# Moving one table-load step of ScalarE from the end of a recurrent-attention and feed-forward kernel to its front

## The chip, the cores and the metric

One NeuronCore of a Trainium2 chip runs the kernel. The metric is the device time of one execution in microseconds. A core has five engines that run side by side, each through its own list of instructions in order: TensorE (PE, matrix products), VectorE (DVE), ScalarE (ACT, functions such as exponential, and copies), GpSimd (POOL, here a few elementwise steps and the issue of most loads) and SyncE (SP, here the issue of stores and of transposing DMAs). Engines wait for each other through semaphores.

## The reference

Two stages. The first is a recurrent attention with a decay for every channel, for 4 batches, 8 heads, 768 steps and 48 channels a head:

```python
for t in range(S):
    cur = np.einsum('bhd,bhe->bhde', u[None] * kt, vt)
    y[:, :, t] = np.einsum('bhd,bhde->bhe', rt, state + cur)
    state = wt[:, :, :, None] * state + np.einsum('bhd,bhe->bhde', kt, vt)
```

The second takes y as x, with 3072 rows (batch and step) and 384 columns, through a gated feed-forward block with 1024 inner channels:

```python
a = x @ w1
b = x @ w2
h = a * b @ w3
return (h @ w_out).astype(np.float32)
```

## The kernel before

The 768 steps are cut into 6 chunks of 128, and the work into 13 units (`UNITS`): unit t is one chunk of one or two batches. Inside a chunk the recurrence becomes matrix products. For that the kernel needs products of decays over many steps, which it forms as exponentials of running sums of logarithms. So each unit t has, on ScalarE, one logarithm and then three or four exponentials:

- `ln_t` (line 401): lw = ln(w), as soon as the unit's w (`win_t`) has landed
- `cs_t` on TensorE (lines 413, 418): running sums of lw, by a product with a triangular matrix of ones; `csT_t` (line 450) the same, transposed, for units 0, 2, 3 and 6
- `pc_t` (line 425), `ne_t` (line 432), and `iw_t` and `e_t` (lines 471, 479) or, for units 0, 2, 3 and 6, `et_t` (line 456): exponentials of these sums or of lw

From these VectorE scales k and r (`KRk_t` line 437, `KRw_t` line 467, `KRr_t` line 483), TensorE or a transposing DMA on SP turns them (`trk_t`, `trr_t`, `dtk_t`, `dtr_t`), TensorE forms the products inside the chunk (`m_t_b`, line 548), VectorE masks them (`msk_t_b`, line 567; for a few, ScalarE copies in `mcp_t_b` and GpSimd or VectorE masks), and TensorE makes y from them and from the state (`yi_t_b` line 593, `ys_t` line 583). VectorE adds the term in u (`yb_t`, line 611), and y is transposed into `xT` (`yt_t` and `xT_t`, or `dty_t_b`).

The feed-forward block of unit t follows: `a_t_g` and `b_t_g` (line 687) are x times w1 and w2, ScalarE copies a out (`asb_t_g`, line 692), VectorE multiplies it by b (`abT_t_g`, line 697), and `o_t_b` (line 703) multiplies by `w34`, which is w3 times w_out, formed once in the kernel (`wt`, `w3Te`, `wm`, `w34e`, lines 364 to 378). `osb_t_b` (line 708) copies the result out and `st_t_b` (line 713) stores it.

No scheduler sets the order of the work. It is written out by hand in `ORDER`: each entry is a step's name and the engine that runs it, and every engine runs its own entries in that order. `warmN@n` entries are n matmuls of zeros (line 301), 59 in all in the first 35 us. `BANKS` says which banks of the matrix-product memory and which buffers each step uses; a step that writes a bank waits until the step that read it before is done. Loads of r, k, v, w and of the weights are issued by GpSimd (line 328 and lines 339 to 354).

ScalarE computes a logarithm or an exponential from a table that must be in place. The program builder puts a table load (`ACT_TABLE_LOAD`, `LoadActFuncSet` in the built program) before each function that the table in place doesn't hold; it bears the line of that function. The table that it picks for a logarithm has no exponential, and the one that it picks for an exponential has no logarithm. Copies need none of their own. The step `table` (line 238) loads, by name, a table that has both. In the kernel before it follows `asb_10_0`, with 13 of ScalarE's 154 steps behind it: all logarithms and exponentials stand ahead of it.

Of the kernel before, what the change touches and what calls it, by code (L numbers as in the profile page):

```python
# [58 lines left out]
sa12_0=0 o11_1=2 so11_0=1 o12_1=3 so11_1=3 o12_0=4 so12_1=1 so12_0=3  # L59
"""  # L60
ORDER = """
zeros@DVE vin_0@SP padr@DVE win_1@POOL rin_0@SP padlw@DVE ones@DVE mask1@DVE kin_0@SP win_0@POOL u@SP kin_1@POOL
win_2@POOL rc_0@DVE LT@POOL rin_2@POOL rin_1@POOL ln_1@ACT warm0@18 cs_1@PE vin_1@POOL kc_0@DVE ln_0@ACT padkr@DVE
I128@POOL w3_0@POOL warm1@7 trw_0@PE cs_0@PE csT_0@PE pc_0@ACT win_3@POOL ne_0@ACT KRk_0@DVE padet@DVE mask@POOL
ln_2@ACT kin_2@POOL et_0@ACT warm4@13 csT_2@PE pc_1@ACT iw_1@ACT trk_0@PE KRw_0@DVE uc@POOL trw_2@PE ne_1@ACT cs_2@PE
rk_1@DVE kin_3@POOL trke_0@DVE pc_2@ACT e_1@ACT rw_1@DVE KRk_1@DVE ne_2@ACT KRr_1@DVE w3_1@POOL warm1@5 kv_1@PE
ruk_1@DVE trr_1@PE rk_0@DVE m_0_0@PE rin_3@POOL trk_1@PE msk_0_0@DVE trke_1@ACT trre_1@ACT wo@POOL wt_1_0@PE ruk_0@DVE
et_2@ACT warm6@1 wt_1_1@PE dg_0@DVE m_1_0@PE vc_0@DVE wt_0_0@PE msk_1_0@DVE dv_0@POOL warm4@1 wt_0_1@PE ln_3@ACT
kv_0@PE win_4@POOL KRw_2@DVE w3Te_0@ACT warm5@3 cs_3@PE rk_2@DVE vin_2@POOL pc_3@ACT warm7@1 csT_3@PE ne_3@ACT
KRk_2@DVE dg_1@DVE warm7@1 trk_2@PE et_3@ACT w3_2@POOL ruk_2@DVE yi_0_0@PE trke_2@DVE dv_1@POOL yi_1_0@PE w3Te_1@DVE  # L70
vin_3@POOL warm7@2 yd_1@PE S_1@DVE KRk_3@DVE warm7@2 m_2_1@PE S_0@DVE mcp_2_1@ACT warm7@1 trk_3@PE ybc_1@DVE wt_3_0@PE
trke_3@ACT warm2@1 wt_3_1@PE maff_2_1@DVE yt_1@PE wt_2_0@PE trw_3@PE yb_0@DVE wt_2_1@PE KRw_3@DVE m_2_0@PE yt_0@PE
mcp_2_0@ACT rk_3@DVE m_3_0@PE xT_1@ACT maff_2_0@POOL m_3_1@PE msk_3_1@DVE w1_1@POOL warm2@7 wm_1@PE msk_3_0@DVE
rin_4@POOL dg_2@DVE wm_0@PE w3Te_3@ACT kin_4@POOL w34e_1@DVE ln_4@ACT wm_3@PE win_5@POOL w3Te_2@DVE Sb_0@ACT
w34e_0@ACT dv_2@DVE w2_1@POOL yi_2_0@PE cs_4@PE Sb_1@DVE kin_5@POOL yi_2_1@PE pc_4@ACT wm_2@PE ne_4@ACT yb_2@DVE
w1_0@POOL e_4@ACT ruk_3@DVE wt_5_0@PE wt_4_0@PE w34e_3@ACT wt_5_1@PE ys_3@PE xT_0@ACT w3Te_5@DVE yt_2@PE rin_5@POOL
yi_3_0@PE dg_3@DVE xT_2@ACT wt_4_1@PE wm_5@PE iw_4@ACT dv_3@DVE vin_4@POOL w3Te_4@ACT yi_3_1@PE a_0_1@PE yb_3@DVE
w34e_5@ACT a_2_3@PE rw_4@DVE w3_3@POOL yt_3@PE KRr_4@DVE a_2_2@PE trr_4@PE rk_4@DVE asb_2_2@ACT w2_0@POOL wm_4@PE
trre_4@DVE asb_2_3@ACT ruk_4@DVE xT_3@DVE kv_3@PE ln_5@ACT win_7@POOL kv_2@PE a_1_1@PE KRk_4@DVE w34e_4@ACT dg_4@DVE
cs_5@PE asb_0_1@ACT trk_4@PE pc_5@ACT S_2@DVE iw_5@ACT win_6@POOL b_0_1@PE T_3@DVE ne_5@ACT b_2_2@PE abT_0_1@DVE  # L80
S_3@POOL b_3_2@PE e_5@ACT KRk_5@DVE kin_6@POOL a_3_2@PE asb_1_1@ACT abT_2_2@DVE Sb_2@ACT b_1_1@PE asb_3_2@ACT
rin_6@POOL b_2_3@PE abT_1_1@DVE trke_4@ACT a_1_0@PE abT_2_3@DVE m_4_0@PE abT_3_2@DVE m_4_1@PE mcp_4_0@ACT a_3_0@PE
rw_5@DVE a_0_0@PE KRr_5@DVE asb_1_0@ACT Sb_3@DVE trr_5@PE msk_4_1@DVE maff_4_0@POOL asb_0_0@ACT a_2_1@PE a_3_3@PE
trre_5@DVE win_8@POOL asb_2_1@ACT rk_5@DVE ys_4@PE trk_5@PE dv_4@DVE vin_5@POOL yi_4_0@PE trke_5@ACT wt_6_0@PE
yi_4_1@PE a_3_1@PE yb_4@DVE rin_7@POOL wt_6_1@PE b_0_0@PE ruk_5@DVE kin_7@POOL w3Te_6@DVE b_1_0@PE dty_4_0@SP
abT_0_0@DVE b_2_1@PE win_9@POOL abT_1_0@DVE asb_3_1@ACT wt_7_0@PE dty_4_1@SP wm_6@PE ln_7@ACT abT_2_1@DVE dg_5@DVE
asb_3_0@ACT b_3_0@PE w34e_2@ACT ln_6@ACT vin_6@POOL b_3_1@PE abT_3_0@DVE asb_3_3@ACT wt_7_1@PE abT_3_1@DVE cs_6@PE
kv_4@PE pc_6@ACT ne_6@ACT m_5_1@PE T_4@DVE rin_8@POOL a_2_0@PE msk_5_1@DVE iw_7@ACT csT_6@PE asb_2_0@ACT b_3_3@PE
KRk_6@DVE cs_7@PE w3Te_7@DVE win_10@POOL trk_6@PE pc_7@ACT w34e_6@DVE ne_7@ACT b_2_0@PE trke_6@DVE S_4@POOL a_4_1@PE
et_6@ACT abT_3_3@DVE trw_6@PE abT_2_0@DVE e_7@ACT kin_8@POOL b_4_0@PE KRw_6@DVE asb_4_1@ACT ys_5@PE rk_6@DVE m_5_0@PE  # L90
ln_8@ACT m_6_0@PE win_11@POOL msk_5_0@DVE wm_7@PE mcp_6_0@ACT iw_8@ACT rw_7@DVE vin_7@POOL cs_8@PE KRr_7@DVE yi_5_0@PE
w34e_7@ACT a_4_0@PE dv_5@DVE pc_8@ACT ne_8@ACT rin_9@POOL a_4_3@PE ruk_6@DVE asb_4_0@ACT yi_5_1@PE o_0_0@PE Sb_4@DVE
abT_4_0@DVE yb_5@DVE ln_9@ACT vin_10@POOL o_2_0@PE asb_4_3@ACT dg_6@DVE e_8@ACT rin_10@POOL o_3_0@PE osb_0_0@DVE
iw_9@ACT rk_7@DVE st_0_0@SP dtr_7@SP rw_8@DVE kin_9@POOL yt_5@PE osb_3_0@ACT b_4_1@PE osb_2_0@DVE xT_5@ACT ruk_7@DVE
st_3_0@SP kv_6@PE KRr_8@DVE kv_5@PE m_6_1@PE abT_4_1@DVE maff_6_0@POOL ys_6@PE ln_10@ACT a_5_2@PE dtr_8@SP T_5@DVE
b_4_3@PE vin_9@POOL S_5@DVE asb_5_2@ACT msk_6_1@DVE yi_6_0@PE st_2_0@SP a_5_3@PE win_12@POOL a_5_1@PE T_6@DVE
asb_5_3@ACT KRk_8@DVE cs_9@PE KRk_7@DVE yi_6_1@PE dtk_8@SP a_4_2@PE abT_4_3@DVE vin_8@POOL b_5_3@PE rk_8@DVE
asb_5_1@ACT dv_6@DVE b_5_1@PE ln_11@ACT o_3_1@PE pc_9@ACT iw_10@ACT yb_6@DVE kin_10@POOL ne_9@ACT abT_5_3@DVE yt_6@PE
b_4_2@PE dg_7@DVE asb_4_2@ACT a_5_0@PE e_9@ACT abT_5_1@DVE rin_12@POOL trk_7@PE xT_6@DVE asb_5_0@ACT b_5_0@PE rw_9@DVE
# [18 lines left out]
asb_9_2@ACT st_6_1@SP abT_9_3@DVE st_7_1@SP dtk_12@SP b_9_1@PE osb_8_1@ACT ys_11@PE abT_9_1@DVE st_7_0@SP m_11_0@PE  # L118
m_11_1@PE dtr_12@SP ruk_12@DVE o_8_0@PE msk_11_0@DVE b_9_2@PE msk_11_1@DVE yi_11_0@PE b_10_3@PE osb_8_0@DVE a_10_0@PE
dg_12@DVE a_10_2@PE abT_9_2@DVE yi_11_1@PE dv_12@POOL a_10_3@PE yb_11@DVE a_10_1@PE dty_11_1@SP b_10_1@PE asb_10_1@ACT  # L120
b_10_2@PE asb_10_3@ACT asb_10_2@ACT dty_11_0@SP abT_10_3@DVE o_9_1@PE abT_10_1@DVE asb_10_0@ACT st_8_0@SP table@ACT
m_12_0@PE osb_9_1@DVE m_12_1@PE ys_12@PE msk_12_0@DVE o_9_0@PE msk_12_1@DVE b_10_0@PE b_11_2@PE abT_10_2@DVE
yi_12_0@PE a_11_2@PE b_11_0@PE asb_11_2@ACT yi_12_1@PE osb_9_0@ACT a_11_0@PE yb_12@DVE b_11_3@PE abT_10_0@DVE
dty_12_0@SP a_11_1@PE abT_11_2@DVE b_11_1@PE asb_11_1@ACT dty_12_1@SP o_10_0@PE asb_11_0@ACT st_9_0@SP o_10_1@PE
osb_10_0@ACT a_12_1@PE osb_10_1@DVE a_12_3@PE abT_11_1@DVE st_10_1@SP st_8_1@SP b_12_1@PE abT_11_0@DVE st_10_0@SP
st_9_1@SP a_11_3@PE b_12_0@PE asb_11_3@ACT b_12_2@PE asb_12_1@ACT abT_11_3@DVE asb_12_3@ACT a_12_2@PE b_12_3@PE
asb_12_2@ACT a_12_0@PE abT_12_2@DVE o_11_0@PE abT_12_3@DVE asb_12_0@ACT abT_12_0@DVE o_11_1@PE abT_12_1@DVE
osb_11_0@ACT st_11_0@SP o_12_1@PE osb_11_1@DVE st_11_1@SP o_12_0@PE osb_12_1@ACT st_12_1@SP osb_12_0@ACT st_12_0@SP
"""


# [631 lines left out]
```

## Time and profile before

| | |
|---|---|
| time, median of 3 runs | 186.27 us (185.09 to 186.48) |
| profiled execution, its own time | 186.57 us |
| its span, first to last instruction | 184.8 us |
| TensorE busy | 165.1 us (89%) |
| VectorE busy | 135.1 us (73%) |
| ScalarE busy | 115.3 us (62%) |
| GpSimd busy | 82.6 us (45%) |
| table loads on ScalarE | 21, of 1283 ns each |

Busy times are sums over the span; the span and the time differ by what lies before the first and after the last instruction. An instruction's idle time is the time that its engine stood still just before it, and the releaser is what ended that wait. In groups and timelines, L401 is line 401 of the kernel.

### The profile page before, as it was taken

What the parts mean: (1) busy time and instruction counts of PE and PEld (TensorE: products, weight loads), DVE (VectorE), ACT (ScalarE), POOL (GpSimd) and SP (SyncE); (2) the same over time, 40 slices, a digit from 0 to 9 for tenths busy, and PEclk for the clock granted to TensorE, in tenths of its full rate; (3) what the DMA queues carried; (4) which work ended last, traced back from release to release, by engine and by line L of the source; (5) the groups of instructions that cost most, each with busy time, mean ns of one, the idle gap of its engine ahead of it and who ended that gap; (6) DMA issues with size and microseconds to landing.
All of it is one profiled execution on the core that took longest, in us unless ns stands there. A gap on an engine that the chain in (4) does not pass through costs nothing.

```text
span 184.8 us, 4729 instructions
## 1 busy us (share of the span) xinstructions
PE 165.1 (89%) x1981; PEld 122.4 (66%) x1985; DVE 135.1 (73%) x219; ACT 115.3 (62%) x174; POOL 82.6 (45%) x82
## 2 busy tenths in 40 slices
PE   7997769979989996989699999599999969999992
PEld 2454446548778975856478878377678848797860
DVE  4425976758868977897989898489998867751560
ACT  2387985399698479899969748945433410723421
POOL 7997470998252986998703020031277103000000
PEclk9999999999999999999969999999999999999999
DMA  5999999999999999999999929053499993303413
GB/s 120 220 167 203 175 227 189 82 184 188 171 227 190 121 135 148 173 169 143 192 142 176 168 49 161 1 142 63 112 65 135 62 273 101 85 4 85 170 55 117
DMA packets 99669, 25.83 MB, mean 140 GB/s; under 512 B 91712, under 2 KB 97472, under 8 KB 99648
## 3 DMA queue, kind: packets, MB, share of 16 engines
q0 software_dynamic: 76320, 15.96, 98.3%
q1 hardware_dynamic: 23328, 9.57, 25.6%
q8 instruction: 15, 0.25, 0.6%
q14 instruction: 6, 0.05, 0.1%
HBM read 27.98 MB, written 4.72 MB: 177 GB/s over the span
## 4 chain that ended last, share of the span: by engine, by line
PE 58%; ACT 24%; DMA 7%; issue 5%; DVE 2%; POOL 1%; SPq 0%; ACTq 0%; DVEq 0%; POOLq 0%
PE banks L687 26%; PE banks L703 14%; ACT L401 4%; DMA win<-in_w_dram 4%; DMA out_dram<-osb 4%; ACT a_sb L692 3%; PE banks L548 3%; ACT lw L401 3%; PE banks L593 2%; PE banks L301 2%; PE banks L373 2%; PE banks L413 2%; ACT NEt L432 2%; ACT L425 1%; ACT ETt L456 1%
## 5 line engine op out<-in xcount | busy, mean ns | idle before, releaser
L687 PE MATMUL banks<-xT,w_bf 128*128 128x256 bf16 (+1 forms) x624 | 71.2, 268 | 0.7 <-ACT Et L479 0.7
L687 PEld LDWEIGHTS <-w_bf 128*128 128x128 bf16 x624 | 55.8, 99 | 8.4 <-issue 1.1
L692 ACT COPY a_sb<-banks 128x512 f32<-128x512 f32 x48 | 27.3, 590 | 32.0 <-PE banks L687 25.0
L697 DVE TENSOR_TENSOR abT<-a_sb,banks 128x512 bf16<-128x512 f32 x48 | 31.8, 682 | 10.5 <-ACT a_sb L692 6.9
L703 PE MATMUL banks<-w,abT 128*128 128x384 bf16 x192 | 33.9, 326 | 0.9 <-ACT w L378 0.9
L703 PEld LDWEIGHTS <-abT 128*128 128x128 bf16 x192 | 18.2, 98 | 11.7 <-issue 0.9
L567 DVE TENSOR_TENSOR Mbf<-banks,mask 128x1024 bf16<-128x1024 f32 x19 | 22.7, 1220 | 3.1 <-PE banks L548 3.0
L536 POOL TENSOR_TENSOR dv<-vin,dg 128x768 bf16<-128x768 bf16 (+1 forms) x7 | 9.1, 1294 | 35.3 <-DVE dg L527 21.0
L301 PE MATMUL banks<-zeros 128*128 128x512 bf16 x59 | 17.9, 431 | 1.6 <-DVE zeros L242 1.2
L708 ACT COPY osb<-banks 128x384 f32<-128x384 f32 x17 | 7.9, 479 | 14.5 <-PE banks L703 11.5
L328 POOL DMA_DIRECT2D win<-in_w_dram x13 | 15.0, 1153 | 3.8 <-ACT lw L401 1.9
L611 DVE TENSOR_TENSOR yb<-banks,dv 128x768 bf16<-128x768 f32 (+1 forms) x12 | 11.1, 922 | 6.2 <-PE banks L593 3.2
L328 POOL DMA_DIRECT2D rin<-in_r_dram x12 | 13.8, 1154 | 1.0 <-DVE rk L517 1.0
L328 POOL DMA_DIRECT2D kin<-in_k_dram x12 | 14.0, 1164 | 0.2 <-issue 0.2
L328 POOL DMA_DIRECT2D vin<-in_v_dram x12 | 13.8, 1147 | 0.3 <-issue 0.3
L401 ACT ACTIVATE lw<-win 128x768 bf16<-128x768 f32 (+1 forms) x13 | 10.3, 795 | 5.4 <-DMA win<-in_w_dram 5.3
L401 ACT ACT_TABLE_LOAD x10 | 12.8, 1283 | 1.4 <-PEq L747 0.8
L662 POOL TENSOR_TENSOR Sst<-Tst,pc 128x384 f32<-128x384 f32 x4 | 3.7, 918 | 19.7 <-DVE Tst L654 19.7
L301 PEld LDWEIGHTS <-zeros 128*128 128x128 bf16 x63 | 6.3, 107 | 8.3 <-issue 3.5
L527 DVE TENSOR_REDUCE dg<-ruk 128x16 f32<-128x768 bf16 (+1 forms) x13 | 11.4, 884 | 0.0
L373 PE MATMUL banks<-wo_bf,w3T 128*128 128x384 bf16 x64 | 11.4, 326 | 0.0
L548 PE MATMUL banks<-KRT 64*128 64x128 bf16 x192 | 8.3, 217 | 3.1 <-ACT a_sb L692 2.2
(89 smaller groups left out, 242.7 us busy)
## 6 DMA issues: line engine op xcount, KB each, us to landing
out_dram<-osb SPq DMA_DIRECT2D x24, 192.0 KB, 2.1
win<-in_w_dram POOLq DMA_DIRECT2D x11, 384.0 KB, 8.3
rin<-in_r_dram POOLq DMA_DIRECT2D x11, 192.0 KB, 9.6
kin<-in_k_dram POOLq DMA_DIRECT2D x11, 192.0 KB, 7.6
vin<-in_v_dram POOLq DMA_DIRECT2D x11, 192.0 KB, 9.3
w_bf<-in_moe_w_dram POOLq DMA_DIRECT2D x4, 512.0 KB, 9.6
w_bf<-in_moe_w_dram POOLq DMA_DIRECT2D x4, 384.0 KB, 8.7
wo_bf<-in_moe_w_out_dram POOLq DMA_DIRECT2D x1, 768.0 KB, 12.5
```

Source lines behind the costliest of these rows:

```text
L301: nc.tensor.matmul(banks[:, at, :], lhsT=zeros[:, :C], rhs=zeros, start=True, stop=True)
L328: QUEUE[eng].dma_start(dst, src)
L373: nc.tensor.matmul(one(f"wm{fi}")[:, :DM], lhsT=w3T[fi % 2][:, gi, :], rhs=wo_bf[:, gi, :], start=(gi == 0), stop=(gi == FI - 1))
L401: nc.scalar.activation(LW[:, :, :D], ww, Act.Ln)
L527: nc.vector.reduce_sum(dgs, ruks, axis=AX.X)
L548: nc.tensor.matmul(o[:, e, q, :], lhsT=KRTs[a:a + PAD, 0, b * HP + q, :], rhs=KRTs[a:a + PAD, 1, b * HP + q, :], start=True, stop=True)
L567: nc.vector.tensor_mul(Mbf[bank[f"M{t}_{b}"]], mview(), mask.rearrange("s (j q) t -> s j q t", j=2))
L611: nc.vector.tensor_add(ybs.rearrange("t b (q e d) -> t e (b q) d", e=2, d=D), yview().rearrange("t e (x d) -> t e x d", d=D), dvs.rearrang ...
L687: nc.tensor.matmul(o[:, f, :], lhsT=wt[:, di, fi * P:(fi + 1) * P], rhs=x[:, di, :T], start=(di == 0), stop=(di == DI - 1))
L692: copier(eng)(a_sb[bank[f"sa{t}_{g}"]], one(f"a{t}_{g}"))
L697: nc.vector.tensor_mul(ab[:, g * per:(g + 1) * per, :T], sa.rearrange("p (f t) -> p f t", t=T), one(f"b{t}_{g}").rearrange("p (f t) -> p f ...
L703: nc.tensor.matmul(one(f"o{t}_{b}")[:, :DM], lhsT=ab[:, fi, b * C:(b + 1) * C], rhs=w34[:, fi, :], start=(fi == 0), stop=(fi == FI - 1))
```

## The change

One entry of `ORDER`, `table@ACT`, moves from between `st_8_0@SP` and `m_12_0@PE` to the very front. No other entry changes place; the rest of the diff is the same text with its line breaks shifted.

```diff
 ORDER = """
-zeros@DVE vin_0@SP padr@DVE win_1@POOL rin_0@SP padlw@DVE ones@DVE mask1@DVE kin_0@SP win_0@POOL u@SP kin_1@POOL
-win_2@POOL rc_0@DVE LT@POOL rin_2@POOL rin_1@POOL ln_1@ACT warm0@18 cs_1@PE vin_1@POOL kc_0@DVE ln_0@ACT padkr@DVE
+table@ACT zeros@DVE vin_0@SP padr@DVE win_1@POOL rin_0@SP padlw@DVE ones@DVE mask1@DVE kin_0@SP win_0@POOL u@SP
+kin_1@POOL win_2@POOL rc_0@DVE LT@POOL rin_2@POOL rin_1@POOL ln_1@ACT warm0@18 cs_1@PE vin_1@POOL kc_0@DVE ln_0@ACT
...
-b_10_2@PE asb_10_3@ACT asb_10_2@ACT dty_11_0@SP abT_10_3@DVE o_9_1@PE abT_10_1@DVE asb_10_0@ACT st_8_0@SP table@ACT
-m_12_0@PE osb_9_1@DVE m_12_1@PE ys_12@PE msk_12_0@DVE o_9_0@PE msk_12_1@DVE b_10_0@PE b_11_2@PE abT_10_2@DVE
+b_10_2@PE asb_10_3@ACT asb_10_2@ACT dty_11_0@SP abT_10_3@DVE o_9_1@PE abT_10_1@DVE asb_10_0@ACT st_8_0@SP m_12_0@PE
+osb_9_1@DVE m_12_1@PE ys_12@PE msk_12_0@DVE o_9_0@PE msk_12_1@DVE b_10_0@PE b_11_2@PE abT_10_2@DVE yi_12_0@PE
...
```

In the built programs the lists of TensorE, VectorE, GpSimd and SyncE are the same. ScalarE's list differs in its table loads alone. Before there are 21: ten at line 401, six at line 425, two at line 479, and one each at lines 456, 471 and 238. After there is one, at line 238, as ScalarE's first instruction. The line of each source statement stays the same.

## The prediction

> **What bounds the kernel now.** The page comes first: TensorE is busy for 165.1 of 184.8 us, and ScalarE's busiest slices are the ones in which TensorE's digit falls.
>
> ```profile
> PE 165.1 (89%) x1981; PEld 122.4 (66%) x1985; DVE 135.1 (73%) x219; ACT 115.3 (62%) x174; POOL 82.6 (45%) x82
> PE   7997769979989996989699999599999969999992
> ACT  2387985399698479899969748945433410723421
> PEclk9999999999999999999969999999999999999999
> ```
>
> One slice is 4.6 us. From slice 3 to slice 24 ScalarE is mostly at 8 or 9 tenths and TensorE mostly below its full 9; after 120 us ScalarE falls to 1 to 5 tenths and TensorE stays full. So there are two regimes: up to about 120 us ScalarE holds TensorE up at places, after it TensorE sets the time alone.
>
> Then ScalarE's groups, shapes kept apart, for what it does there (line, engine, operation, count; busy us, mean ns; idle before).
>
> ```profile
> L401 ACT ACT_TABLE_LOAD x10 | 12.8, 1283 | 1.4 <-PEq L747 0.8 <-DMA win<-in_w_dram 0.5
> L425 ACT ACT_TABLE_LOAD x6 | 7.7, 1283 | 0.1
> L479 ACT ACT_TABLE_LOAD x2 | 2.6, 1283 | 0.0
> L456 ACT ACT_TABLE_LOAD x1 | 1.3, 1283 | 0.0
> L471 ACT ACT_TABLE_LOAD x1 | 1.3, 1283 | 0.0
> L238 ACT ACT_TABLE_LOAD x1 | 1.3, 1283 | 0.0
> ```
>
> Twenty-one loads, 26.9 of ScalarE's 115.3 us. They stand wherever a logarithm (L401) follows an exponential or the other way round; L238 is the step that is moved.
>
> Third, TensorE's waits, of which the four longest on ScalarE are these (total us, times, longest).
>
> ```profile
> PE banks L548 <- ACT a_sb L692: 2.2, 1, 2.2
> PE banks L413 <- ACT lw L401: 1.8, 3, 1.1
> PE banks L413 <- ACT w L378: 1.1, 1, 1.1
> PE banks L462 <- ACT ETt L456: 1.1, 1, 1.1
> ```
>
> The timeline shows what stands behind the first of them.
>
> ```profile
> 114.63 1.28 ACT L401 ACT_TABLE_LOAD   x1
> 115.92 0.84 ACT L401 ACTIVATE lw<-win 128x768 bf16<-128x768 f32 x1
> 116.67 0.46 ACT L708 COPY osb<-banks 128x384 f32<-128x384 f32 x1
> 117.15 1.28 ACT L479 ACT_TABLE_LOAD   x1
> 118.45 0.81 ACT L479 ACTIVATE Et<-banks 128x768 bf16<-128x768 f32 x1
> ...
> 119.79 0.40 PE L548 MATMUL banks<-KRT 64*128 64x128 bf16 x8 [2.16 <-ACT a_sb L692]
> ```
>
> Two loads stand within 4 us, ScalarE runs without a pause, and TensorE idles 2.16 us until the copy behind them has emptied a bank. On the chain that ended last, table loads stand at twelve places and take 14.1 us (11.19, 13.35, 20.78, 23.84, 37.05, 48.93, 51.94, 66.48, 80.83, 84.61, 87.24 and 117.15 us): a ceiling, since other work comes up as they go.
>
> **What the change does to the instructions.** In the built programs ScalarE has 21 loads before and one after; nothing else moves on any engine, and no DMA or queue is touched. The load at 0.79 us is replaced by the joint one in the same place, also 1283 ns by the L238 row. It is hidden by the 4.01 us that ScalarE idles before 6.09 us for win; without that cover it would cost 1.28. The load at 159.61 lies ahead of a 3.22 us wait for TensorE (to 164.12): nothing. So 19 loads, 19 x 1.283 = 24.4 us of ScalarE, lie where they can matter. A load starts only after the wait of the instruction it serves (at 11.19 ScalarE first waits 0.46 for win), so idle time before it doesn't hide it.
>
> **What each stretch gives.** I go by TensorE's idle times as the timeline puts them, and ask at each whether ScalarE, without its loads and with TensorE already early by the sum so far, is done in time.
>
> To 20 us: idle 0.19 (13.38) and 1.06 (15.29, for et_0). Without the loads ln_2 runs 11.2 to 12.0 when win lands, and et_0 ends at 12.6 instead of 15.24; the warm matmuls keep TensorE until 13.19. Both go: 1.25. The 0.67 at 19.40 stays: there ScalarE itself had waited 1.07 for TensorE.
>
> 20 to 34: 0.16 and 0.49 before cs_3 and 0.92 at 26.06 (for ne_3) go; of 0.56 at 26.98 (for et_3) 0.21 goes, since et_3 itself (1.03) follows ne_3 directly; 0.47 at 32.63 stays (the copy waited for TensorE). 1.78, together 3.03.
>
> 34 to 60: 1.07 at 39.85 (w34e_0 behind the load at 37.05), 0.15 (51.12), 0.71 (55.60), 0.14 (57.89). With loads gone at 37.05, 39.82, 48.93 and 51.94 ScalarE is early by 5 us at e_5. 2.07, together 5.10.
>
> 60 to 92: 1.15 (70.26, ln_6), 0.55 (72.93, ne_6), 0.85 (83.39, w34e_7 behind 80.83), 0.59 (89.39, e_8 behind 87.24), 1.02 (91.20, xT_5). Six loads, 7.7 us, leave a ScalarE that is without a pause from 66.5 to 91.2 but for 0.69. All go; 0.23 at 79.96, ended by VectorE, stays. 4.16, together 9.26.
>
> 92 to 118: TensorE has no idle time, so loads at 97.55 and 114.63 give nothing by themselves. Two things meet here. The granted clock is at half for 3.4 us:
>
> ```profile
> 90.00:100.00 10.00, 8.98 (x100) 6.93 (x95) 8.73 (x14) 8.12 (x13) 1.91 (x3) 0.83 1.65 166
> ```
>
> The three closing columns are granted clock, DMA share and GB/s: 0.83 over 10 us is 1.7 us of matmul time lost (twelve 128x256 matmuls take 2.41 at 91.49, 1.47 at 75.00). It follows three idle times within 8 us that the change removes, so up to 1.7 may come back. Against it, VectorE idles only 1.00 (84.62) between 75.3 and 96.9, so it is early by 6.7 + 1.0 = 7.7 where TensorE is early by 9.26: TensorE would wait up to 1.3 for msk_6_1 ahead of yi_6_0 (93.69 before). VectorE then has 5.44 us of idle (0.87, 0.37, 0.81, 0.62, 2.77) to catch up by 119.3. Between -1.7 and +1.3 I take 0.
>
> By the Trainium skill ("TensorE: Matmul & The Clock Gate", section "HAM oscillation — how this bites in real kernels") the clock falls after idle gaps of over about 3.4 us. The trace differs: the longest idle time in the 20 us before 91.88, where the clock falls, is 1.02. By that rule the half-clock stretch has another cause and may stay; the sum, which counts no clock, would be the same and its lower end 1.7 higher.
>
> At 119.79 the 2.16 go: without 2.57 us of loads osb_5_1, e_10 and asb_7_0 end ahead of TensorE. Together 11.42.
>
> After 120: TensorE's 1.18 (150.00, a transposing DMA) and 0.32 (150.98, a copy behind a store) stay. Nothing.
>
> The sum: 11.4 us. Profiled execution 186.57 (span 184.8 and 1.8 around it, unchanged) - 11.4 = 175.2; the median shown is 0.3 lower, so 174.9.
>
> **Loads from memory** could stop this, since the load queue's packets fill 98.3% of the engines' time. Even with no landing earlier than now it holds: w2's second half lands at 46.2 and is first read at 52.1 (5.9 to spare, 4.25 needed there), w2's first half 56.2 and 63.9 (7.7, needed 5.1), win_6 60.0 and 69.4 (9.4, needed 5.1 to 6.3).
>
> **Rivals.**
> VectorE takes the bound from 75 us on and doesn't give it back: the gain stops at 6.8 + 1.0 = 7.8, 178.5 us. For it: 9 tenths in many slices from 60 to 140 us. Against: its later idle times wait for TensorE or ScalarE, which both come earlier.
>
> Stores and transposing DMAs on SP come forward by 9 to 11 us, into the stretch where the load queue is still busy (last landing 107.8 in that run of loads). A KR transpose issue takes 2.99 at 94.95 and 1.24 at 108.77; a store lands in 6.85 at 143.52 against a median of 2.1. One such landing more on the path costs 4.75: 179.6. Against: the transposes of units 8 and 9 (issued at 94.95 to 110.72) are first read from 119.79 and 132.29 on, over 20 us later.
>
> On the other side: logarithm and exponential are slower out of the joint table, of which no row here has one. Lines 401, 425, 432, 456, 471 and 479 spend 40.2 us in 59 activations. Were each twice as long, ScalarE would have 40.2 - 24.4 = 15.8 us more, and at the 11.4 / 24.4 = 0.47 that a microsecond of ScalarE is worth above, the kernel would be 7.4 slower: 193.7. It decides from 61% longer (24.4 / 40.2). Against: 768 elements take 845 ns as logarithm and as exponential (L401, L471) from two different tables, so the shape sets it.
> The Trainium skill ("ScalarE activation tables: per-element evaluation and per-set limits", section "What a function is on this engine") says that the same operands cost the same whichever table is read, and the two rows agree; by that rule this rival has no chance.
>
> That the loads stay: the built program has none left, so 186.3 only if the order of instructions didn't hold on the chip.
>
> **How the numbers follow.** Forecast 0.70, VectorE 0.15, SP's DMAs 0.10, slower activations 0.02, loads stay 0.01, the rest spread over smaller gains 0.02. Range: down to 174.9 - 1.7 (clock back in full) - 0.4 (what is left at 26.98) = 172.8, up past both rivals to 180.5. Faster by over 1% (what a measurement here can tell from no change, 1.9 us) 0.95; within 1% 0.03; slower 0.02.
>
> **What would show it.** One table load on ScalarE and 24 to 26 us less busy time; logarithm and exponential still near 845 ns; TensorE's waits on ScalarE down from 13.1 to under 3 us; the 2.16 before L548 gone; no half-clock slice near 90 us. It is wrong if TensorE's total idle stays over 12 us, if VectorE's tiles (KR, Mbf, abT) head its waits, or if lw, NEt or Et rows have grown.

## The result, and the profile after

| | before | after |
|---|---|---|
| median (range) of 4 runs each | 185.81 us (185.09 to 186.48) | 178.99 us (177.10 to 180.47) |
| profiled execution: time, span | 186.57, 184.8 us | 180.47, 178.8 us |

The ratio is 0.960, with a 95% interval of 0.950 to 0.970: faster, by some 7 us where the prediction had 11.4. Here and below, medians and ranges are of all executions, while a ratio leaves out those more than 1.5% above the fastest of their kernel. The time lies inside its range (172.8 to 180.5), nearer to the rivals' times (178.5 and 179.6) than to the forecast's 174.9. The profiled execution is the longest of its four, so its losses are at the upper end of what this kernel loses.

The page of the changed kernel, in the same lines as before (engines; busy tenths in 40 slices of 4.5 us; granted clock; the two DMA queues with packets, MB and share of the 16 engines):

```profile
PE 163.7 (92%) x1981; PEld 121.6 (68%) x1985; DVE 133.8 (75%) x219; ACT 89.0 (50%) x154; POOL 82.5 (46%) x82
PE   7998998999999997999999799919999889999991
ACT  2255853586774578964791774222623312232431
PEclk9999999999999999999999999996999999999999
q0 software_dynamic: 76320, 15.96, 103.4%
q1 hardware_dynamic: 23328, 9.57, 30.5%
```

ScalarE is busy 26.3 us less and is no longer at 9 tenths for long. But TensorE has a new hole: slice 26, from 116 to 121 us, holds a 1 where before there was a 9, and the slice of half clock has moved behind it. TensorE's waits and VectorE's (total us, times, longest) name the hole:

```profile
PE banks L703 <- ACT osb L708: 3.8, 1, 3.8
PE banks L687 <- DMA xT<-yb: 1.4, 2, 1.2
...
PE banks L630 <- DVE yb L611: 1.1, 1, 1.1
```

```profile
DVE rw L475 <- DMA rin<-in_r_dram: 4.5, 1, 4.5
...
DVE KR L437 <- DMA kin<-in_k_dram: 1.3, 1, 1.3
```

The timeline of that stretch (start, us, engine, line, tiles; in brackets the idle time before it and what ended it) shows how one leads to the other:

```profile
115.34 1.46 PE L703 MATMUL banks<-w,abT 128*128 128x384 bf16 x8
118.32 0.56 DVE L475 TENSOR_TENSOR rw<-rin,iw 128x768 bf16<-128x768 bf16 x1 [4.51 <-DMA rin<-in_r_dram]
118.80 1.02 DVE L437 TENSOR_TENSOR KR<-kin,NEt 128x768 bf16<-128x768 bf16 x2
...
119.38 0.81 ACT L432 ACTIVATE NEt<-banks 128x768 bf16<-128x768 f32 x1 [4.89 <-DVE KR L437]
...
120.09 0.47 ACT L708 COPY osb<-banks 128x384 f32<-128x384 f32 x1
...
120.61 0.65 PE L703 MATMUL banks<-w,abT 128*128 128x384 bf16 x3 [3.81 <-ACT osb L708]
```

`rw_11` waits for `rin_11`, a load from memory. `KRk_10` stands behind it on VectorE, `ne_12` on ScalarE waits for `KRk_10` (its buffer), `osb_2_1` stands behind `ne_12`, and TensorE needs the bank that `osb_2_1` empties. The wait list says "ACT osb", as it did before the change for other waits; the chain says DMA.

How early each matmul starts against the same matmul before tells where the gain is made and where it goes. Start before minus start after, in us, medians of the matmuls near the point, by the time before:

| time before | 40 | 60 | 80 | 93.7 | 106 | 114 | 126 | 130 | 134 | 170 |
|---|---|---|---|---|---|---|---|---|---|---|
| after | 5.1 | 6.6 | 6.9 | 11.1 | 11.7 | 9.7 | 11.9 | 7.9 | 6.3 | 6.1 |

Up to 126 us the change gives 11.9; then 5.6 is lost within 8 us and stays lost. (Two microseconds are lost already between 106 and 114; at 119.8 the wait of 2.16 us that is gone makes up for them.)

The load queue shows why `rin_11` is late. Issue, landing and first read of that load and of `kin_9`, in us:

| | `kin_9` | `rin_11` |
|---|---|---|
| before | 79.7, 90.2, 108.1 | 90.6, 107.8, 125.7 |
| after | 76.2, 97.8, 97.8 | 98.1, 118.3, 118.3 |

The loads land not earlier but later, while the reads come forward. Landings stand still from 84.0 to 91.5, 91.5 to 97.8, 102.3 to 107.8 and 112.4 to 118.3 us. SyncE's queue (SPq) issues the transposing DMAs of units 7 to 10 (L488, L503) ahead of these landings (the seventh, at 119.37, is behind them):

```profile
78.88 1.40 SPq L488 DMA_TRANSPOSE KRT<-KR  x1
...
81.50 2.54 SPq L488 DMA_TRANSPOSE KRT<-KR  x1
...
84.76 4.10 SPq L503 DMA_TRANSPOSE KRT<-KR  x1
...
98.57 1.29 SPq L503 DMA_TRANSPOSE KRT<-KR  x1
...
100.65 2.44 SPq L488 DMA_TRANSPOSE KRT<-KR  x1
...
108.72 1.24 SPq L488 DMA_TRANSPOSE KRT<-KR  x1
```

They land at 86.1, 92.3, 97.6, 107.4, 109.9 and 115.0 us. Before, the first three were issued at 87.94, 91.58 and 94.95 us, with one long still stretch (93.0 to 103.7, broken by one landing at 99.2), and the other three at 108.77 or later, when the loads were through (107.8).

A second thing adds to it. GpSimd's timeline, which issues the loads:

```profile
84.32 1.14 POOL L328 DMA_DIRECT2D rin<-in_r_dram  x1 [1.01 <-DVE Tst L654]
91.83 1.14 POOL L328 DMA_DIRECT2D kin<-in_k_dram  x1 [6.37 <-DMA rin<-in_r_dram]
98.13 1.14 POOL L328 DMA_DIRECT2D rin<-in_r_dram  x1 [5.16 <-PE banks L413]
99.29 1.49 POOL L536 TENSOR_TENSOR dv<-vin,dg 128x768 bf16<-128x768 bf16 x1
```

`kin_11` is issued 0.3 us after `rin_10` has landed (91.5), and `rin_11` 0.3 us after `kin_9` (97.8): each time the load seven places earlier. So late landings hold back the next issue, and `dv_7`, GpSimd's own work, behind it. From 68.7 us on, twelve issues of the changed kernel start this way; in the kernel before only two of these loads do (84.95 and 86.25). (At 98.13 the timeline names TensorE as the releaser; by the landings it is `kin_9`, as 6 us earlier it was `rin_10`.)

**Theory.** The gain on ScalarE is as forecast; some 5 to 6 us of it are lost because the transposing DMAs come forward into the stretch in which the load queue is busy, and loads then land too late. **Rivals:** the loads are merely wanted earlier, whatever SP does, and their order decides; the earlier or the later half of the table loads gives less than it was priced at; or the half clock is what costs.

### The profile page after: what moved, and what is told of

Its sections match the earlier page's. It is cut to its first block, busy times and chain, and to the rows that moved or that the text cites. A ratio compares the mean times of both kernels' runs of the same rounds, so it can differ in the third digit from the quotient of the medians.

```text
span 178.8 us, 4709 instructions
## 1 busy us (share of the span) xinstructions
PE 163.7 (92%) x1981; PEld 121.6 (68%) x1985; DVE 133.8 (75%) x219; ACT 89.0 (50%) x154; POOL 82.5 (46%) x82
## 3 DMA queue, kind: packets, MB, share of 16 engines
q1 hardware_dynamic: 23328, 9.57, 30.5%
## 4 chain that ended last, share of the span: by engine, by line
PE 63%; DMA 21%; DVE 7%; ACT 3%; issue 2%; SPq 1%; DVEq 0%; ACTq 0%
PE banks L687 22%; PE banks L703 13%; DMA rin<-in_r_dram 11%; PE banks L301 8%; DMA xT<-yb 6%; PE banks L373 5%; DMA out_dram<-osb 4%; PE banks L548 3%; PE banks L593 2%; DVE abT L697 2%; DVE Mbf L567 1%; PE banks L413 1%; PE banks L364 1%; PE banks L583 1%; PE banks L646 1%
## 5 line engine op out<-in xcount | busy, mean ns | idle before, releaser
L687 PE MATMUL banks<-xT,w_bf 128*128 128x256 bf16 (+1 forms) x624 | 70.3, 265 | 1.8 <-DMA xT<-yb 1.4
L703 PE MATMUL banks<-w,abT 128*128 128x384 bf16 x192 | 35.4, 335 | 3.8 <-ACT osb L708 3.8
L328 POOL DMA_DIRECT2D win<-in_w_dram x13 | 14.9, 1148 | 5.1 <-DMA rin<-in_r_dram 1.8
L328 POOL DMA_DIRECT2D kin<-in_k_dram x12 | 13.8, 1154 | 7.2 <-DMA rin<-in_r_dram 6.4
L328 POOL DMA_DIRECT2D rin<-in_r_dram x12 | 14.0, 1165 | 6.9 <-PE banks L413 5.2
L708 ACT COPY osb<-banks 128x384 f32<-128x384 f32 x17 | 8.0, 481 | 16.7 <-PE banks L703 13.9
L328 POOL DMA_DIRECT2D vin<-in_v_dram x12 | 13.7, 1142 | 0.6 <-PE banks L373 0.3
L432 ACT ACTIVATE NEt<-banks 128x768 bf16<-128x768 f32 (+1 forms) x13 | 9.9, 761 | 7.5 <-DVE KR L437 7.5
L527 DVE TENSOR_REDUCE dg<-ruk 128x16 f32<-128x768 bf16 (+1 forms) x13 | 11.4, 883 | 0.0
L373 PE MATMUL banks<-wo_bf,w3T 128*128 128x384 bf16 x64 | 11.4, 326 | 0.0
L437 DVE TENSOR_TENSOR KR<-kin,NEt 128x768 bf16<-128x768 bf16 (+1 forms) x13 | 6.7, 531 | 4.1 <-ACT NEt L432 2.4
## 6 DMA issues: line engine op xcount, KB each, us to landing
wo_bf<-in_moe_w_out_dram POOLq DMA_DIRECT2D x1, 768.0 KB, 11.9
```

The lines of the kernel that those rows point to most:

```text
L328: QUEUE[eng].dma_start(dst, src)
L373: nc.tensor.matmul(one(f"wm{fi}")[:, :DM], lhsT=w3T[fi % 2][:, gi, :], rhs=wo_bf[:, gi, :], start=(gi == 0), stop=(gi == FI - 1))
L432: nc.scalar.activation(dst, cs_view(), Act.Exp, scale=-1.0)
L527: nc.vector.reduce_sum(dgs, ruks, axis=AX.X)
L687: nc.tensor.matmul(o[:, f, :], lhsT=wt[:, di, fi * P:(fi + 1) * P], rhs=x[:, di, :T], start=(di == 0), stop=(di == DI - 1))
L703: nc.tensor.matmul(one(f"o{t}_{b}")[:, :DM], lhsT=ab[:, fi, b * C:(b + 1) * C], rhs=w34[:, fi, :], start=(fi == 0), stop=(fi == FI - 1))
```

## The experiments

Each ratio is against the kernel before, run beside it. Short diffs are against the changed kernel unless another is named; `...` stands for what is left out.

**e1, the changed kernel once more**, unchanged.

> The changed kernel again, as the reference for the other three on the same chip. Theory L (late load): TensorE is early by some 12 us at the place that was 118 us before and loses 4 to 6 of them at o_6_1 and the products after it, because rin_11 lands after 113 us, the time at which rw_11 wants it; 177 to 180.5. Theory C (clock): the loss is the half-clock stretch of 3.4 us, in whatever place it falls; then a run without one is at 174 to 175.5 and rin_11's time doesn't matter.

Median 177.72 us (173.24 to 179.22) against 186.15. In this execution another load was late: `vin_8`, issued at 80.7, landed at 107.1. VectorE's and TensorE's waits:

```profile
DVE dv L536 <- DMA vin<-in_v_dram: 4.0, 1, 4.0
...
```

```profile
PE banks L687 <- DVE Mbf L567: 3.5, 1, 3.5
```

Its matmuls start 14.2 us early at 119.8 and 7.9 at 126: a like loss, in another place. `rin_11`, which was expected to be the late one, landed at 114.9 and was read at 117.3. The best run, 173.24, is below the forecast.

**e2, loads in the order in which they are wanted** (GpSimd's last ten loads ahead of `dv_7`; `rin_11` goes from the tenth place to the sixth):

```diff
-vin_10 rin_10 kin_9 vin_9 win_12 vin_8 kin_10 rin_12 kin_11 rin_11
+kin_9 rin_10 vin_9 win_12 vin_8 rin_11 kin_10 kin_11 rin_12 vin_10
```

> The changed kernel with the last ten loads on GpSimd in the order in which their data are first read (kin_9, rin_10, vin_9, win_12, vin_8, rin_11, kin_10, kin_11, rin_12, vin_10); same loads, same engines. Theory L: rin_11 takes a slot three places earlier and lands by 103 to 108 us, kin_9 by about 90; the waits of VectorE for rin (4.5 us) and kin (1.3 us) go, TensorE keeps its 12 us: 173 to 175.5. Theory C: rin_11's wait was covered, the time stays within 1 us of the changed kernel's, 177 to 180.

176.28 us (175.31 to 180.88), ratio 0.946 (0.941 to 0.951): better, but not all the way to the 173 to 175.5 of theory L. `rin_11` landed at 108.9, and in this stretch no r or k is waited for over 0.3 us any more, but the last load, `vin_10`, has its issue held until 99.72, and `dv_7` behind it, on which VectorE waits:

```profile
DVE yb L611 <- POOL dv L536: 3.0, 1, 3.0
```

**e3, the transposing DMAs of units 7 to 10 as plain copies** of the same bytes. What follows for these units computes on unturned numbers, in the same shapes and steps.

```diff
+    PLAIN = {7, 8, 9, 10}
...
+    def plain(dst, src):
+        nc.sync.dma_start(dst.rearrange("p x t -> p (x t)"), src)
...
-                nc.sync.dma_start_transpose(KRTs[:, 0], KRs[:, 0].rearrange("t h d -> t (h d)"))
+                (plain if t in PLAIN else nc.sync.dma_start_transpose)(KRTs[:, 0], KRs[:, 0].rearrange("t h d -> t (h d)"))
```

> The changed kernel with the seven transposing DMAs of KR of units 7 to 10 replaced by plain copies of as many bytes in the same places of SP's order; k and r of these units are left unturned, so the products that follow work on other numbers. Theory L with the transposes as the cause: the load queue no longer stands still for 6 to 7 us at 84 to 98 and again after 102 us, the last load of the run lands before 105 us instead of 118, no wait for rin on VectorE, 173 to 175.5. If the load queue is simply full, whatever SP does: rin_11 lands after 112 us as before and the time stays at 177 to 180.

174.62 us (173.95 to 176.52), ratio 0.939 (0.933 to 0.946). The DMA part of the page, and the last line of what it has on L328, the line of the loads, for the changed kernel and for this one:

```profile
KRT<-KR SPq DMA_DIRECT2D x7, 256.0 KB, 2.6
...
KRT<-KR SPq DMA_TRANSPOSE x4, 3.3
```

```profile
DMA to landing us min/median/max: 4.3/10.6/26.7
```

```profile
DMA to landing us min/median/max: 4.2/10.7/14.5
```

`rin_11` lands at 101.1 instead of 118.3 us, no load of this stretch is waited for, and matmuls start 12.3 us early at 126 and 12.6 at 170. The copies were issued as early as the transposes had been (77.96, 80.71, 84.39 and 99.10 us and on). So SP's DMAs do this harm not by coming early alone, but because they transpose. By what means a transpose holds the loads up (its further packets or something else) no run here separates.

**e4, the joint table only in the later half** (the table step just ahead of `ln_7`, which stands ahead of `ln_6`; of the twenty other loads the ten ahead of it stay and ten go, not twelve and eight as the expectation has it), and **e5, only in the earlier half** (table in front, and a table with the logarithm alone loaded ahead of `ln_7`):

```diff
-table@ACT zeros@DVE ...
+zeros@DVE ... wm_6@PE table@ACT ln_7@ACT
```

```diff
-... wm_6@PE ln_7@ACT
+... wm_6@PE table2@ACT ln_7@ACT
...
+nc.scalar.preload_act_table_set("natural_log")
```

> The kernel before with the joint table loaded just ahead of ln_7 (at about 66 us): twelve loads stay, eight go. By the prediction's sum the stretches from 66 us on give 4.2 + 2.2 = 6.3 us; TensorE is then at most 6.5 us early at 118 us and rin_11 is wanted at about 119 instead of 113. Theory L: the load is in time or nearly so, so half of the loads' removal gives nearly all that the whole change gives: 179 to 181. If the gain goes by the number of loads (8 of 20, of 7 us): 183.

> The other half: the joint table at the front, and the plain logarithm table loaded again just ahead of ln_7 (about 61 us), from where logarithm and exponential switch as in the kernel before. By the prediction's sum TensorE gains 5.1 us up to 60 us and keeps it: the loads are then wanted about 5 us earlier, not 12. Theory L: nothing is late, about 181. The two halves, 5.3 (measured for the second) and 5.1, then add to more than the 7 to 8 that the whole change gives, the rest being what late loads cost. If the table loads' gain itself had been sized too large (first half below 3.5): 182.5 or more.

e4: 180.89 us against 186.15, 5.3 less, ratio 0.971 (0.966 to 0.976). e5: 179.27 against 185.38, 6.1 less, ratio 0.970 (0.965 to 0.975). Together 11.4 us, the sum that was forecast for the whole; the whole alone gives 6.8 to 8.4 by the medians of its three measurements. The later half gives 5.3 where the sum had 6.3, the earlier one 6.1 where it had 5.1 (179.3 us, below the "about 181" expected). With half of it `rin_11` lands at 108.0 (e4) and 104.8 us (e5) and is read at 119.8 in both, in time. So both halves together are worth the price, and the loss comes only with both: it needs the reads and the transposes far enough forward.

**e6, the plain copies in the kernel before**, and **e7, the load order of e2 in the kernel before**; the same edits, `table` at its old place.

> The kernel before, with the plain copies of the third experiment (KR of units 7 to 10 is copied, not turned; the products that follow work on other numbers). Theory L: without the change the loads of this stretch land 8 to 20 us ahead of their use, so a quicker load queue gives nothing: within 1 us of the kernel before, 185 to 186.5. If the transposing DMAs cost the path directly, whatever the table: 3 us or more off, 183 or less.

> The kernel before with the load order of the second experiment. Theory L: loads there are early in any order; within 1 us of the kernel before. If the order is better by itself: 184 or less.

186.33 us, ratio 1.002 (0.997 to 1.006), and 185.10, ratio 1.001 (0.998 to 1.005): no change clear of noise. What e2 and e3 gained is therefore a loss that the change had brought, and no reserve of the old kernel.

**e8 and e9, the load order with `dv_7` ahead of the held issues.** In both, GpSimd's entries stand in this order (`maff_6_0` left out), `vin_10` last:

```diff
-vin_10 rin_10 kin_9 vin_9 win_12 vin_8 kin_10 rin_12 kin_11 rin_11 dv_7 S_7
+kin_9 vin_8 win_12 rin_10 vin_9 rin_11 kin_10 dv_7 kin_11 rin_12 S_7 vin_10
```

In e8 `S_7` stands ahead of VectorE's `T_7` in `ORDER` and so doesn't wait for it: the state of unit 7 is updated from an older product. In e9 it stands behind `T_7`.

> The changed kernel with the loads by due time (kin_9, vin_8, win_12, rin_10, vin_9, rin_11, kin_10, kin_11, rin_12, vin_10) and GpSimd's dv_7 and S_7 taken out from behind the loads whose issue blocks (in the second experiment vin_10's issue held dv_7 and with it yb_7 for 3 us). Theory L: no wait on a load over 1 us on VectorE; 174 to 175.5. If what is left is the clock and not the loads: 176 or more.

> The eighth experiment with S_7 behind T_7 again, as in the changed kernel, and vin_10 directly behind S_7; there S_7 stood ahead of T_7 and didn't wait for it. Theory L: as the eighth but for S_7's wait, loads late by at most 1 us on VectorE: 174 to 176, below the changed kernel's 177 to 179. If the eighth's time came from the missing wait: 176.5 or more.

174.00 us (172.99 to 176.53), ratio 0.939 (0.932 to 0.945), and 173.92 (172.39 to 174.33), ratio 0.933 (0.928 to 0.938). The loads still land late (`kin_10` at 109.6, `rin_12` at 116.5 us), but in an order in which that hurts little (in e9 VectorE still waits 1.7 us for r, where at most 1 was expected): the loss has a second cure, which leaves the transposes alone.

**e10, two transposes later on SP**, and **e11, the changed kernel again**:

```diff
-ln_10@ACT a_5_2@PE dtr_8@SP T_5@DVE ... yi_6_1@PE dtk_8@SP a_4_2@PE
+ln_10@ACT a_5_2@PE T_5@DVE ... yi_6_1@PE a_4_2@PE
...
-st_3_1@SP b_5_2@PE
+st_3_1@SP dtr_8@SP dtk_8@SP b_5_2@PE
```

> The changed kernel with two transposing DMAs, dtr_8 and dtk_8, moved back in SP's order from before and after st_2_0 to behind st_3_1 (from about 81 to 88 us to about 91 to 95); they are first read at about 108. Load order as in the changed kernel. Theory L: from 84 to 91 us the load queue goes on, the loads up to vin_8 land some 3 to 6 us earlier and the last ones as they do now or 1 to 3 us earlier; 175 to 177.5. If only the sum of the DMA work matters and not where the transposes fall: 177.5 to 179.5.

> The changed kernel once more, beside the last one on the same chip: 177 to 179, with a spread of 3 us or more between executions, since which load comes late differs from one to the next.

e10: 174.96 us (172.89 to 175.55), ratio 0.938 (0.932 to 0.943), a little better than expected. The two now go at 92.5 and 94 us instead of 81.5 and 84.8, and `rin_11` lands at 111.0, 3.3 ahead of its read: moving two DMAs by 10 us in their queue gives back some 3 of the microseconds. e11: 177.87 (176.38 to 180.18), ratio 0.953 (0.947 to 0.958); in its profile VectorE waits 2.7 for r and 1.9 for k. Its executions settle the half clock as a rival: at a mean granted clock of 0.998 to 1.0, with no half-clock stretch, four of them took 176.38, 177.87, 177.87 and 179.49 us, where theory C of e1 had 174 to 175.5 for such a run. In e1 itself the one execution at full clock took 173.24, so e1 alone would not have told.

**e12, e9 and e10 together.**

> The load order and GpSimd order of the ninth experiment and the later transposes of the tenth together. Theory L: what either leaves of late loads goes; the prediction's sum of 11.4 and the half-clock time are then all regained, 172.5 to 174.5. If each had taken away the same waits, no better than the ninth: 173.5 to 175.

172.83 us (172.59 to 173.22), ratio 0.929 (0.925 to 0.933): 13.3 us below the kernel before and 5.0 below the changed one beside it. Engines and clock on its page, then 100 to 120 us in the changed kernel and in this one (busy us by engine PE, PEld, DVE, ACT, POOL; granted clock, DMA share, GB/s):

```profile
PE 162.0 (95%) x1985; PEld 121.1 (71%) x1985; DVE 133.3 (78%) x219; ACT 89.3 (52%) x154; POOL 82.3 (48%) x82
...
PEclk9999999999999999999999999999999999999999
```

```profile
100.00:120.00 20.00, 15.74 (x196) 11.70 (x194) 14.86 (x22) 8.93 (x17) 3.35 (x3) 1.00 1.36 115
```

```profile
100.00:120.00 20.00, 20.00 (x265) 14.82 (x263) 18.50 (x31) 11.40 (x21) 3.41 (x4) 1.00 0.89 140
```

(`ORDER` has 63 matmuls of zeros, not 59 as said at the start; four matmuls are missing in the trace of the changed kernel, hence 1981 and 1985.) TensorE is busy for all of the 20 us, against 15.74. `rin_11` lands at 93.1 and is read at 111.5. Matmuls start 14.1 us early at 126 and 13.9 at 170. The range is 0.6 us wide; that of the changed kernel over its 14 executions in three sessions is 7.2 (173.24 to 180.47). That the width comes from which load is late is what its three profiles suggest (`rin_11`, `vin_8`, then `rin_11` and `kin_9`); but these are of executions near the top of the range (180.47, 178.80 and 180.18), and where the shorter ones lose time no trace shows. That they lose some is plain from the times: the shortest execution of e11, 176.38, is 3.2 us above the longest of e12.

## Why the prediction was right, and where it was not

**In short.** The mechanism of the gain held: ScalarE without its table loads frees about what the sum says. The time of 174.9 did not: 178.99 is 4.1 above it, and it lies in the range only because that reaches up past two rivals, neither of which came true as priced. That is in part luck.

**The gain on ScalarE and TensorE.** 11.42 was the sum at 119.8 us; 11.9 was measured there, and the two halves come to 11.4. By stretch the steps read 1.25, 3.03, 5.10 and 9.26 (20, 34, 60, 92 us), measured 1.9, 3.9, 6.6 and 10.1. By 99 us it is 11.7; that last 1.6 is clock, as the half-clock stretch of the kernel before (91.9 to 95.3) has no like here. TensorE's idle time to 60 us fell by 4.65 (6.79 to 2.14), near the 5.10; of the other 1.9 us, 0.4 lies in the 18 matmuls of zeros at the start, which took 6.25 instead of 6.65 (the full clock was granted at 5.7 instead of 6.5 us), and the rest I have not split. The agreement at 119.8 is part luck: those gains were offset by losses at 103 us of the changed kernel (1.06, in `yb`, behind `kin_9`'s landing and `dv_7`) and at 99 us (0.42). In e12, without late loads, it is 14.1.

**The single steps.** One table load, 26.3 us less on ScalarE (24 to 26 forecast). TensorE's waits on ScalarE are down from 13.1 to 5.3 us, 1.5 without the 3.81; the 2.16 ahead of L548 is gone. The rows of the activations:

```profile
L401 ACT ACTIVATE lw<-win 128x768 bf16<-128x768 f32 x11 | 9.4, 852 | 0.9 <-DMA win<-in_w_dram 0.9
L432 ACT ACTIVATE NEt<-banks 128x768 bf16<-128x768 f32 x11 | 8.9, 810 | 7.5 <-DVE KR L437 7.5
L471 ACT ACTIVATE iw<-lw 128x768 bf16<-128x768 bf16 x8 | 6.8, 850 | 0.0
```

852, 810 and 850 ns against 845, 807 and 845: the joint table is no slower by more than 1%, and the rival on the other side falls.

Two readings in the prediction are off, and little hangs on them. From slice 3 to 24 TensorE is not mostly below 9: it stands at 9 in 14 of the 22. And a table load doesn't always start after the wait of its instruction: those at 0.79 and 8.47 us ran ahead of waits of 4.01 and 0.43 us, so idle time can hide one.

**VectorE takes the bound**: not so. The gain was to stop at 7.8 from 75 us on; it went to 11.7 at 106.

**The step that failed** is "Loads from memory could stop this ... Even with no landing earlier than now it holds". Landings equal to those before was meant as the worst case and was not: `rin_11` landed 10.5 us later, `kin_9` 7.7 later. And only w2 and `win_6` were followed, up to 70 us. Had the landings stayed, the sentence would have been true: `rin_11` at 107.8 against a read at about 114.

**SP's DMAs**, the rival given 0.10, had the mechanism: transposes come forward into the stretch where the load queue is busy. It looked for the cost in the wrong place, a store that lands late (4.75), and weighed it by when the transposes are read, "over 20 us later", not by what they do to the loads. Its 179.6 is near the 178.99 by a different sum: in the profiled execution 5.8 are lost behind 126 us where it had 4.75, 3.81 as wait, about 1.8 as clock and 0.2 as others.

**The half clock.** The stretch near 90 us is gone, as forecast, but one of the same length (3.4 us, 121.8 to 125.2) follows the 3.81 us wait. Of the 5.6 lost between 126 and 134, 3.8 is the wait and 1.8 the clock, so the 1.7 that "may come back" came back near 92 us and was lost again. In e12, with no idle time over 1.0 behind the start, the clock is full to the end of the work.
The Trainium skill ("TensorE: Matmul & The Clock Gate", section "HAM oscillation — how this bites in real kernels") has the clock fall after idle gaps of over about 3.4 us. The 3.81 here fits that; other traces do not. In e11 the same stretch of 3.4 us follows a gap of 2.03; in e1 the clock falls at 110.1, only 2.3 us into the gap of 3.54; in the kernel before it falls after 0.85, 0.59 and 1.02, and in e7, with the same three gaps in the same place, it doesn't.
What the traces have in common is a grid. Counted from the first full clock of an execution, every half-clock stretch starts a whole number of 3.41 us later (34 of them in the changed kernel: 5.73 + 34 x 3.413 = 121.8). In the 14 traces seven stretches begin ahead of the end of the work, and TensorE's idle time in the 3.41 us just before each is 2.33 (e1), 2.25 (changed), 2.03 (e11), 1.87 (e6), 1.61 (before), 1.61 (e5) and 1.58 us (e2). No grid step at full clock with 1.57 us of idle time or less was followed by half clock; three with 1.62 to 1.67 were not either (e7, e5, e11). In e7 the 0.59 and the 1.02 fall into two steps. So the place of the idle time on the grid decides along with its length, and the prediction's "three idle times within 8 us" was not the whole cause.

**TensorE's idle time over the span** is 15.1 us (178.8 - 163.7) after 19.7; the prediction called itself wrong from 12 on, and the 3.81 alone carries it over (15.1 - 3.8 = 11.3).

## What to carry to other kernels

When a change takes work off the bound engine, everything behind it comes forward, and that includes DMAs on other queues: for each load still in flight, ask what newly overlaps it, and take "lands as now" for a hope and not for a worst case. A wait list names the engine that was last in a chain; follow the chain back until it ends in something that nobody in it was late for. A kernel whose executions spread wider than those of the old one (7.2 us against 4.1, 184.33 to 188.47, here) may have a transfer that is late now and then; an order by due time, GpSimd's own work ahead of held issues, and two DMAs moved back were worth 5.0 us on top of the change.

## What the runs showed of the hardware

- A transposing DMA holds up loads that GpSimd has issued; a plain copy of the same bytes does so far less. With seven transposes made copies the longest load falls from 26.7 to 14.5 us, and the hardware queue has 16,944 packets instead of 23,328, 912 fewer for each.
- From 68 us on at most seven loads were in flight here (up to eight around the weights' loads): a further one was issued 0.3 us after the landing of the one seven places earlier (91.5 and 91.8, 97.8 and 98.1; in e1 91.3 and 91.6, 92.9 and 93.2), and what stood behind it on GpSimd waited too, `dv_7` until 99.3.
- Half clock came in steps of 3.41 us on a grid that starts with the first full clock, and followed a step at full clock in which TensorE was idle for 1.58 us or more (seven cases in 14 traces); it never followed 1.57 or less, and with 1.62 to 1.67 it stayed away three times.
